# Attention and two feed-forward stages in one kernel: blocks in product order, sums last in a step, conversions in two calls, next-stage loads from the third product

## The chip, the cores and the metric

The kernel runs on one core of a Trainium2 chip. The metric is the device time of one execution in microseconds. Three runs of the kernel before gave 1167.41, 1167.29 and 1166.38 us; the median is 1167.29.

## The reference

Attention with normalised q and k over 4 x 12 heads of 448 x 64, then two feed-forward stages on the same 1792 tokens of width 768. All weights of the two stages are given in double precision (float64).

```python
q_n, k_n = (rmsnorm(q, g_q), rmsnorm(k, g_k))
scores = scale * np.matmul(q_n, k_n.transpose(0, 1, 3, 2))
scores = scores - np.max(scores, axis=-1, keepdims=True)
attn = np.exp(scores)
attn = attn / (np.sum(attn, axis=-1, keepdims=True) + 1e-09)
x = np.matmul(attn, v)                      # then (1792, 768)
# stage 0: w_in 768 x 2048, w_out 2048 x 768
h = np.maximum(x @ w_in, 0.0)
x = (h * h) @ w_out
# stage 1: w_gate and w_val 768 x 1536, w_out 1536 x 768
g = x @ w_gate
silu = g * (1.0 / (1.0 + np.exp(-g)))
out = (silu * (x @ w_val)) @ w_out
```

## The kernel before

After the attention come four stages of matmuls: up 0 and down 0 (the two matrices of the first feed-forward stage), up 1 and down 1. In each, a product of two block matrices is made from seven block products P1 to P7 in place of eight (Strassen's scheme, in the form of Winograd), with sums and differences of blocks on both sides. Every 32-bit block is split into a high and a low half of the fp32r type, and a block product is three matmuls: high by high, high by low, low by high.

- **up(ph)** works in steps of 9 matmuls. A step is one product, one pair of hidden blocks q_ and one half of the tokens (tp). q_ = 0 and 1 are interleaved (28 steps), later q_ take 14 steps each, in the order P1, (P4 of the one before), P5, P6, P2, P7, P3. up 0 has 112 steps, up 1 168.
- **down(ph)** goes through the products in the order P2, P5, P3, P1, P6, P7, P4, each over ng blocks of the hidden width (ng is 8 in stage 0 and 6 in stage 1), with 18 matmuls per block n. At a product's last block its six banks are copied or added out (L1301 for copies).
- **Weight blocks** go through a ring of five buffers (`ring`; in the trace without numbers, in the order of instructions as ring_82 to ring_86). stream() makes them: ACT casts the high half (L494), DVE subtracts for the low half (L267). Sums of blocks that a product needs are made in `ssum`, `conv` or in place (plus L270, minus L267).
- **Conversions**: weights arrive as 768 KB slabs of double-precision words (loads, L250, in three regions of xacc) and are turned into 32-bit floats by convert(): one ACT instruction (L291), a TENSOR_SCALAR (L292) and two SCALAR_TENSOR_TENSOR (L264) on DVE. Quads feed up stages. Slabs for a down stage ("keep") are converted during the up stage, stored to memory (`wkeep`, L354) and fetched back by bring() (dn<-wkeep, L363); some ("area") are converted straight into `dn` when the down stage has begun.
- **Hidden blocks**: finished sums are stored by send_part() (hid<-xacc, L1018), in the down stages fetched by stage() (dn<-hid, L1224) and split by cleave(): ACT the high half (L1237), DVE the low half (L1059, xat or xab<-dn). sum_of() makes further sums of hidden blocks on DVE (L1059, xacc<-xacc).
- **Order on an engine** is the order of emission; each engine runs its queue in order. After each step, pump(rate) issues conversions (C), blocks (B) and low halves that are due (L) until a budget of DVE time is spent. run_due() runs what later() has planned; load_raws() issues loads up to `state["limit"]`. At the start of up 0 a table given to plan_types() places splits ("h" ACT L146, "l" DVE L150) and combines ("c" L127) of the two token pairs' input blocks. All DMAs here are issued by SP's queue, in order.

## Time and profile before

| | |
|---|---|
| median of three runs | 1167.29 us |
| lowest and highest | 1166.38 and 1167.41 us |
| the profiled execution, its own time | 1166.46 us |
| its span | 1164.4 us |
| mean granted clock of TensorE | 0.988 of full speed |
| PE busy | 1127.7 us (97%) |
| DVE busy | 869.5 us (75%) |
| ACT busy | 636.9 us (55%) |
| POOL busy | 213.0 us (18%) |
| slabs loaded (w_in, w_out, w_gate, w_val) | 16, 28, 12, 12 (768 KB each) |
| wkeep stores and reads | 23 and 23 (384 KB each) |

The profile comes from one execution, whose own time is near the lowest of the three runs; the span leaves out some 2 us around it. w_out stands for both second matrices. PE is busy nearly all the time, so the time lies in the few places where PE stands still, or runs its matmuls at a lower clock, and in what it waits for there. The column PEclk of a window is the granted clock as a share of full speed.

### The profile page before, as it was taken

To read this page: it belongs to the slowest core of one execution; us is meant where nothing else is said; L and a number is where in the kernel's file an instruction comes from. 1 tells how busy PE (TensorE), PEld (TensorE's weight loads), DVE (VectorE), ACT (ScalarE), POOL (GpSimd) and SP (SyncE) were. 2 spreads that over 40 slices of the span, in tenths; PEclk is the share of its full clock that TensorE was granted. 3 is DMA by queue.
4 is the path that set the end of the run, shared out by engine and by line. 5 is a ranking of instruction groups with operands and counts; after the bars stand their busy time and mean duration, and the time that the engine had idled before them with its cause. 6 is when DMAs were issued, how large, how long until landed. Compare 5 with 4: busy or idle time off the path is not lost.

```text
span 1164.4 us, 17032 instructions
## 1 busy us (share of the span) xinstructions
PE 1127.7 (97%) x6164; PEld 953.7 (82%) x6164; DVE 869.5 (75%) x1253; ACT 636.9 (55%) x1047; POOL 213.0 (18%) x220
## 2 busy tenths in 40 slices
PE   7999999999799999789999999999999999999998
PEld 5555555569699899679999999999999899898997
DVE  7777888679878887789456787979787784765554
ACT  6887877667566665554444546443443434245332
POOL 5899999741000000000000000000000000000000
PEclk9999999999999999899999999999999999999999
DMA  6444332111978778984444401755464551764553
GB/s 172 122 123 125 97 97 60 47 33 35 323 238 266 248 245 281 355 292 143 127 127 127 127 17 51 242 173 194 146 219 144 185 183 50 279 231 131 174 177 136
DMA packets 116739, 190.38 MB, mean 164 GB/s; under 512 B 13616, under 2 KB 97584, under 8 KB 116656
## 3 DMA queue, kind: packets, MB, share of 16 engines
q1 hardware_dynamic: 116336, 189.30, 50.5%
q8 instruction: 48, 0.79, 0.3%
q14 instruction: 35, 0.29, 0.1%
q10 hardware_dynamic: 320, 0.00, 0.0%
HBM read 129.50 MB, written 59.59 MB: 162 GB/s over the span
## 4 chain that ended last, share of the span: by engine, by line
PE 74%; DVE 10%; DMA 9%; ACT 3%; issue 2%; SPq 1%; POOL 0%; ACTq 0%; DVEq 0%; POOLq 0%
PE ps L1097 31%; PE ps L1278 25%; PE s L750 6%; PE s L765 6%; DMA dn<-wkeep 3%; DVE xacc L1059 3%; PE s L721 2%; DVE conv L264 2%; PE s L689 2%; PE s L786 2%; DMA hid<-xacc 2%; DMA dn<-hid 1%; DMA xacc<-in_moe_w_out_dram 1%; DVE ring L267 1%; ACT xacc L1062 1%
## 5 line engine op out<-in xcount | busy, mean ns | idle before, releaser
L1097 PE MATMUL ps<-xb,ring 128*128 128x448 f32 x1080 | 231.7, 371 | 9.9 <-DVE ring L267 9.1
L1097 PEld LDWEIGHTS ps<-xb,ring 128*128 128x128 f32 x1080 | 205.4, 191 | 29.7 <-DVE ring L267 11.7
L1278 PE MATMUL ps<-xat,ring 128*128 128x448 f32 x1008 | 211.0, 372 | 11.1 <-DVE xat L1059 5.9
L1278 PEld LDWEIGHTS ps<-xat,ring 128*128 128x128 f32 x1008 | 192.6, 192 | 29.4 <-DVE xat L1059 7.9
L1278 PE MATMUL ps<-xab,ring 128*128 128x448 f32 x756 | 155.9, 368 | 2.8 <-ACT xacc L1301 1.8
L1097 PE MATMUL ps<-xat,ring 128*128 128x448 f32 x720 | 156.1, 366 | 0.8 <-DVE ring L267 0.8
L1278 PEld LDWEIGHTS ps<-xab,ring 128*128 128x128 f32 x756 | 143.0, 190 | 15.5 <-ACT xacc L1301 2.2
L1097 PEld LDWEIGHTS ps<-xat,ring 128*128 128x128 f32 x720 | 135.0, 188 | 12.5 <-DVE ring L267 1.1
L1062 ACT ACTIVATE xacc<-ps 128x448 f32<-128x448 f32 x148 | 79.3, 543 | 102.7 <-PE ps L1097 95.4
L264 DVE SCALAR_TENSOR_TENSOR conv<-xacc,conv 128x768 int32<-128x768 int32 x126 | 121.5, 965 | 3.3
L1062 ACT ACTIVATE xacc<-xacc 128x448 f32<-128x448 f32 x148 | 84.8, 577 | 68.9 <-DVE xacc L1059 66.7
L1097 PE MATMUL ps<-xab,ring 128*128 128x448 f32 x540 | 116.3, 366 | 0.0
L1059 DVE TENSOR_TENSOR xacc<-ps,xacc 128x448 f32<-128x448 f32 x164 | 98.5, 619 | 20.0 <-PE ps L1097 14.5
L724 DVE TENSOR_REDUCE mxz<-s 112x2 f32<-112x896 f32 x96 | 100.2, 1088 | 16.4 <-PE s L721 16.1
L1097 PEld LDWEIGHTS ps<-xab,ring 128*128 128x128 f32 x540 | 101.3, 188 | 8.8 <-issue 0.7
L1237 ACT CAST xat<-dn 128x896 fp32r<-128x896 f32 x56 | 52.8, 943 | 96.3 <-PE ps L1278 66.0
L1059 DVE TENSOR_TENSOR xat<-dn,xat 128x896 fp32r<-128x896 f32 x56 | 61.0, 1089 | 55.3 <-ACT xat L1237 55.0
L756 POOL TENSOR_TENSOR sg<-p 112x896 f32<-112x896 f32 x46 | 96.8, 2106 | 15.1 <-ACT p L752 15.1
L752 ACT ACTIVATE p<-s 112x896 f32<-112x896 f32 x96 | 87.8, 919 | 20.4 <-PE s L750 16.1
L267 DVE TENSOR_TENSOR ring<-conv,ring 128x384 fp32r<-128x384 f32 x127 | 69.7, 559 | 30.2 <-ACT ring L494 30.1
L1059 DVE TENSOR_TENSOR xacc<-xacc 128x448 f32<-128x448 f32 x148 | 87.6, 620 | 4.5 <-DMA hid<-xacc 4.0
L1059 DVE TENSOR_TENSOR xab<-dn,xab 128x896 fp32r<-128x896 f32 x42 | 45.8, 1090 | 52.4 <-ACT xab L1237 52.4
(97 smaller groups left out, 1353.4 us busy)
## 6 DMA issues: line engine op xcount, KB each, us to landing
hid<-xacc SPq DMA_DIRECT2D x196, 224.0 KB
dn<-hid SPq DMA_DIRECT2D x98, 448.0 KB
xacc<-in_moe_w_out_dram SPq DMA_DIRECT2D x28, 768.0 KB
xacc<-in_moe_w_in_dram SPq DMA_DIRECT2D x16, 768.0 KB
xacc<-in_moe_w_gate_dram SPq DMA_DIRECT2D x12, 768.0 KB
xacc<-in_moe_w_val_dram SPq DMA_DIRECT2D x12, 768.0 KB
wkeep<-conv SPq DMA_DIRECT2D x23, 384.0 KB
dn<-wkeep SPq DMA_DIRECT2D x23, 384.0 KB
```

Source lines behind the costliest of these rows:

```text
L264: nc.vector.scalar_tensor_tensor(out=out, in0=in0, scalar=scalar, in1=out, op0=op, op1=ALU.bitwise_or)
L267: nc.vector.tensor_tensor(out=out, in0=a, in1=b, op=ALU.subtract)
L724: nc.vector.tensor_reduce(out=mxz[:, c, 0:P:D], in_=ps[:CP, :, :S], op=ALU.max, axis=AX.X)
L750: nc.tensor.matmul(ps[:CP, a, :S], lhs, rhs, start=(w == 0), stop=(w == 3))
L752: nc.scalar.activation(out=p, in_=ps[:CP, :, :S], func=AF.Exp)
L756: nc.gpsimd.tensor_tensor(out=sg, in0=p_t[pi, 2 * w], in1=p_t[pi, 2 * w + 1], op=ALU.add)
L765: nc.tensor.matmul(ps[s, :S], v_t[pi][:, a, c * D:(c + 1) * D], p[:, a, :], start=(c == 0), stop=(c == NCH - 1),)
L1059: eng.tensor_tensor(out=o, in0=a, in1=b, op=op)
L1062: nc.scalar.activation(out=slot(s), in_=src, func=func)
L1097: nc.tensor.matmul(ps, w[:, wi, kk * P:(kk + 1) * P], xk[:, xi, kk * S:(kk + 1) * S], start=bool(first and mm == 0), stop=(mm == 3 * KT - ...
L1237: nc.scalar.copy(k[:, 0], src)
L1278: nc.tensor.matmul(ps_of(ps[tp, o]), w[:, wi, o * P:(o + 1) * P], h[:, hi, tp * S:(tp + 1) * S], start=bool(first and m == 0), stop=(g == ...
```

## The change

It changes the order in which work is issued, and which slabs are kept.

- In stage 0 the kept even slabs are one (0) instead of three (0, 2, 4), so 9 slabs are stored and brought instead of 11, and slabs 2 and 4 become area slabs. The table `more`, by which kept slabs are spread over q_, changes with it.
- The limit of the loads: in up 0 all loads of stage 0 are open from the first step (before, after the table of splits is done); in down 0 the loads of the next stage's first quads (four) are open from block 2 x ng on, the first of the third product.
- convert() issues the TENSOR_SCALAR one call of pump later than the ACT part.
- stream() makes P6's block before P2's, as the products use them.
- Sums by sum_of() are issued at the end of a step, after pump.
- In a down stage, at a product's last block the evictions are issued ahead of pump and of the low half of the hidden block n + 2. bring() asks for slabs up to n + 7 in place of n + 5.
- The table of plan_types for up 0 has the splits of T3 and B21 of pair two ahead of those of T4 of pair one.

```diff
@@ -199,14 +199,15 @@
     loads, limits, jobs, kepts = [], [], [], []
     for ph in range(2):
         nq = len(ups[ph])
-        kept = list(range(1, NF[ph], 2)) + list(range(0, (6, NF[1])[ph], 2))
+        kept = list(range(1, NF[ph], 2)) + list(range(0, (2, NF[1])[ph], 2))
         kepts.append(list(kept))
-        more = ({4: 1, 7: 4}, {7: 1, 11: 1})[ph]
+        more = ({2: -1, 5: 1, 6: 1, 7: 2}, {7: 1, 11: 1})[ph]
 
         def job(what, a, b, src):
             jobs.append((ph, what, a, b, len(loads)))
             loads.append(src)
 
+        limits.append(len(loads))
         for n, (w, g) in enumerate(ups[ph]):
             if n == 2:
                 limits.append(len(loads))
@@ -289,8 +290,10 @@
             high, low = two[:, :, 1], two[:, :, 0]
         ci = c.bitcast(I32)
         yield act(lambda: nc.scalar.activation(out=c, in_=high.bitcast(F32), func=AF.Copy, scale=TINY))
+        t = state["tick"]
         yield dve(0.56, lambda: nc.vector.tensor_scalar(
-            out=ci, in0=ci, scalar1=3, scalar2=0x7FFFFFFF, op0=ALU.logical_shift_left, op1=ALU.bitwise_and))
+            out=ci, in0=ci, scalar1=3, scalar2=0x7FFFFFFF, op0=ALU.logical_shift_left, op1=ALU.bitwise_and),
+            soft=lambda: state["tick"] > t)
         yield dve(0.97, stt, ci, high, -0x80000000, ALU.bitwise_and)
         yield dve(0.97, stt, ci, low, 29, ALU.logical_shift_right)
         turned[i] = clock["n"]
@@ -440,8 +443,8 @@
                     yield dve(0.55, minus, a21, a11, a21)
                     yield from block((ph, "P5", q_), s_, "s")
                     yield dve(0.55, minus, a11, a22, a21, gate=idle_(key(q_, "a11")))
+                    yield from block((ph, "P6", q_), a11, key(q_, "a11"))
                     yield from block((ph, "P2", q_), a12, key(q_, "a12"), since=lambda: -1)
-                    yield from block((ph, "P6", q_), a11, key(q_, "a11"))
                     yield from block((ph, "P7", q_), a21, key(q_, "a21"), since=lambda: -1)
                     yield dve(0.55, minus, a12, a12, a11, gate=idle_(key(q_, "a12")))
                     yield from block((ph, "P3", q_), a12, key(q_, "a12"), done=over(q_, 0))
@@ -1006,6 +1009,14 @@
         def later(n, fn, *args):
             due.append((clock["n"] + n, fn, args))
 
+        sums_due = []
+
+        def run_sums():
+            now = [d for d in sums_due if d[0] <= clock["n"]]
+            sums_due[:] = [d for d in sums_due if d[0] > clock["n"]]
+            for _, args in now:
+                sum_of(*args)
+
         def run_due():
             now = [d for d in due if d[0] <= clock["n"]]
             due[:] = [d for d in due if d[0] > clock["n"]]
@@ -1052,7 +1063,7 @@
                                      ("T2", ("B22", "T1"), 3 + end), ("T4", ("B21", "T2"), 2)):
                 if new not in when and all(x in when for x in needs):
                     t = when[new] = max(when[x] for x in needs) + wait
-                    later(t - now, sum_of, ph, g, tp, new)
+                    sums_due.append((t, (ph, g, tp, new)))
                     later(t - now + 3, send_part, ph, g, tp, new)
 
         def tt(eng, o, a, b, op=ALU.add):
@@ -1166,6 +1177,7 @@
                 cleave(tp, 0)
                 stage(ph, 2 + tp)
             pump(rate)
+            run_sums()
             if last and p == "P4":
                 cleave(tp, 1)
 
@@ -1188,8 +1200,7 @@
             run_types()
             for p, q_, tp in todo:
                 step(ph, p, q_, tp, 1.2, q_ == last)
-                if not types:
-                    state["limit"] = len(loads) if ph else limits[1]
+                state["limit"] = len(loads) if ph else limits[2]
                 if q_ == last and tp == 1:
                     level = {"P1": 0, "P6": 1, "P2": 2, "P3": 3, "P7": 4, "P4": 5}.get(p)
                     if level is not None:
@@ -1261,7 +1272,7 @@
                 w = ring[at[ph, p, -1 - g] % RING]
                 h = hbuf[n % 3]
                 if n == ng - 1:
-                    assert not due
+                    assert not due and not sums_due
                     free.clear()
                 if n < ng and not state["third"] and all(s in free for s in (3, 4, 5, 6)):
                     claim_third()
@@ -1286,8 +1297,9 @@
                 cleave(n + 2, 0)
                 run_due()
                 stage(ph, n + 4)
-                pump(rate / 2)
-                cleave(n + 2, 1)
+                if g < ng - 1:
+                    pump(rate / 2)
+                    cleave(n + 2, 1)
                 if g == ng - 1:
                     if ph == 0 and p == "P6":
                         assert not waiting((0, 1))
@@ -1312,11 +1324,17 @@
                                 i, j = {"P1": (0, 0), "P6": (0, 1), "P7": (1, 1), "P4": (1, 0)}[p]
                                 k_, t = i * KT + o, 2 * tp + j
                                 nc.sync.dma_start(out=out[k_ * P:(k_ + 1) * P, t * S:(t + 1) * S], in_=d)
-                bring(ph, n + 5)
+                bring(ph, n + 7)
+                if ph == 0 and n == 2 * ng:
+                    state["limit"] = limits[3]
                 load_raws()
                 for fn in plan.get(n, ()):
                     fn()
+                if g == ng - 1:
+                    cleave(n + 2, 1)
+                    pump(rate / 2)
                 pump(rate / 2)
+                run_sums()
             if ph == 0:
                 dn.clear()
                 xb.close()
@@ -1335,8 +1353,8 @@
             (0, "h", 1, "B11", None), (0, "l", 1, "B11", None), (1, "c", 1, "T1", None), (1, "h", 1, "T1", None),
             (2, "l", 1, "T1", None), (3, "h", 0, "T2", None), (4, "l", 0, "T2", None), (5, "h", 1, "B22", None),
             (6, "l", 1, "B22", None), (7, "c", 1, "T3", None), (8, "c", 1, "T2", None), (9, "h", 1, "T2", None),
-            (10, "l", 1, "T2", None), (10, "h", 0, "T4", None), (11, "l", 0, "T4", None), (12, "h", 1, "T3", None),
-            (13, "l", 1, "T3", None), (14, "h", 1, "B21", None), (15, "l", 1, "B21", None), (16, "c", 1, "T4", None),
+            (10, "l", 1, "T2", None), (10, "h", 1, "T3", None), (11, "l", 1, "T3", None), (12, "h", 1, "B21", None),
+            (13, "l", 1, "B21", None), (14, "c", 1, "T4", None), (15, "h", 0, "T4", None), (16, "l", 0, "T4", None),
             (17, "h", 1, "T4", None), (18, "l", 1, "T4", None),
         ])
         up(0)
```

The first place is on DVE at the start of up 0, where xb and xat are split halves of the input blocks and ring_85, ring_86 and ring_82 the blocks of steps 5 and later. Right ahead of the first row stands another subtraction in the kernel before, and the L150 split of xb in the changed one. Before:

```order
L267 TENSOR_TENSOR conv_76<-conv_77 128x384
L150 TENSOR_TENSOR xb_3387<-xacc,xb_3387 128x1344
L267 TENSOR_TENSOR ring_85<-ssum,ring_85 128x384
L267 TENSOR_TENSOR ssum<-conv_76 128x384
L267 TENSOR_TENSOR conv_79<-conv_78,conv_79 128x384
L267 TENSOR_TENSOR conv_78<-conv_79 128x384
L150 TENSOR_TENSOR xb_3387<-xacc,xb_3387 128x1344
L810 RECIPROCAL sp<-sp 56x16
L267 TENSOR_TENSOR ring_86<-ssum,ring_86 128x384
L267 TENSOR_TENSOR ssum<-conv_78 128x384
L150 TENSOR_TENSOR xat<-xacc,xat 128x1344
L267 TENSOR_TENSOR ring_82<-ssum,ring_82 128x384
```

The same place in the changed kernel:

```order
L268 TENSOR_TENSOR conv_76<-conv_77 128x384
L268 TENSOR_TENSOR ring_85<-ssum,ring_85 128x384
L268 TENSOR_TENSOR ssum<-conv_76 128x384
L150 TENSOR_TENSOR xb_3386<-xacc,xb_3386 128x1344
L813 RECIPROCAL sp<-sp 56x16
L268 TENSOR_TENSOR conv_79<-conv_78,conv_79 128x384
L268 TENSOR_TENSOR conv_78<-conv_79 128x384
L268 TENSOR_TENSOR ring_86<-ssum,ring_86 128x384
L268 TENSOR_TENSOR ssum<-conv_78 128x384
L150 TENSOR_TENSOR xat<-xacc,xat 128x1344
L127 TENSOR_TENSOR xacc<-xacc 128x1344
L268 TENSOR_TENSOR ring_82<-ssum,ring_82 128x384
```

The subtractions that stood ahead of a split now stand between it and the low half of the ring, and a combine (L127) stands ahead of ring_82.

The second place is on DVE at steps 24 to 30 of up 0; ring_83 is P6's block, ring_84 P2's, conv_77 a slab in conversion. Before:

```order
L1059 TENSOR_TENSOR xacc<-xacc 128x448 x3
L267 TENSOR_TENSOR conv_80<-conv_76 128x384
L1059 TENSOR_TENSOR xacc<-xacc 128x448 x2
L267 TENSOR_TENSOR ring_82<-ssum,ring_82 128x384
L1059 TENSOR_TENSOR xacc<-xacc 128x448 x3
L292 TENSOR_SCALAR conv_77<-conv_77 128x768
L264 SCALAR_TENSOR_TENSOR conv_77<-xacc,conv_77 128x768 x2
L1059 TENSOR_TENSOR xacc<-xacc 128x448 x2
L267 TENSOR_TENSOR ring_84<-conv_80,ring_84 128x384
L292 TENSOR_SCALAR conv_78<-conv_78 128x768
L264 SCALAR_TENSOR_TENSOR conv_78<-xacc,conv_78 128x768
```

The same place in the changed kernel:

```order
L268 TENSOR_TENSOR conv_80<-conv_76 128x384
L1070 TENSOR_TENSOR xacc<-xacc 128x448 x2
L268 TENSOR_TENSOR ring_82<-ssum,ring_82 128x384
L294 TENSOR_SCALAR conv_77<-conv_77 128x768
L265 SCALAR_TENSOR_TENSOR conv_77<-xacc,conv_77 128x768 x2
L1070 TENSOR_TENSOR xacc<-xacc 128x448 x5
L268 TENSOR_TENSOR ring_83<-conv_80,ring_83 128x384
L1070 TENSOR_TENSOR xacc<-xacc 128x448 x3
L268 TENSOR_TENSOR ring_84<-conv_80,ring_84 128x384
L1070 TENSOR_TENSOR xacc<-xacc 128x448 x2
```

The low half of ring_82 and the conversion move ahead of the sums, ring_83's low half comes ahead of ring_84's, and the conversion of conv_78 falls behind both.

The third place is on DVE in down 1, from block 2 to block 5; `plus` makes the sums in ssum and conv for P5's blocks, and xab<-dn is the low half of a hidden block. Before:

```order
L270 TENSOR_TENSOR conv_80<-dn 128x384
L1059 TENSOR_TENSOR xab<-dn,xab 128x896
L267 TENSOR_TENSOR ring_84<-ssum,ring_84 128x384
L1059 TENSOR_TENSOR xacc<-xacc 128x448
L1059 TENSOR_TENSOR xab<-dn,xab 128x896
L267 TENSOR_TENSOR ring_85<-conv_80,ring_85 128x384
L1059 TENSOR_TENSOR xab<-dn,xab 128x896
L270 TENSOR_TENSOR ssum<-dn 128x384
L1059 TENSOR_TENSOR xab<-dn,xab 128x896
```

The same place in the changed kernel:

```order
L271 TENSOR_TENSOR conv_78<-dn 128x384
L1070 TENSOR_TENSOR xab<-dn,xab 128x896
L268 TENSOR_TENSOR ring_84<-ssum,ring_84 128x384
L1070 TENSOR_TENSOR xacc<-xacc 128x448 x2
L271 TENSOR_TENSOR ssum<-dn 128x384
L1070 TENSOR_TENSOR xab<-dn,xab 128x896
L268 TENSOR_TENSOR ring_85<-conv_78,ring_85 128x384
L1070 TENSOR_TENSOR xacc<-xacc 128x448
L271 TENSOR_TENSOR conv_78<-dn 128x384
L1070 TENSOR_TENSOR xab<-dn,xab 128x896
```

The plus into ssum moves ahead by two of the low halves (xab<-dn), and another plus follows ahead of the next.

## Rows read from the trace of the kernel before

**Rows 1.** The page, part 1: busy time of each engine.
```profile
PE 1127.7 (97%) x6164; PEld 953.7 (82%) x6164; DVE 869.5 (75%) x1253; ACT 636.9 (55%) x1047; POOL 213.0 (18%) x220
```
**Rows 2.** Windows: length, busy time (instructions) of each engine, PEclk, DMA share, GB/s.
```profile
285.00:325.00 40.00, 33.31 (x149) 29.38 (x148) 29.82 (x49) 24.65 (x46) 0.00 (x0) 0.91 0.85 288
...
467.00:515.00 48.00, 36.94 (x151) 31.38 (x150) 36.15 (x51) 25.48 (x40) 0.00 (x0) 0.86 1.01 352
...
900.00:950.00 50.00, 47.55 (x228) 43.63 (x227) 38.01 (x63) 19.87 (x37) 0.00 (x0) 0.97 0.52 166
1002.00:1055.00 53.00, 50.20 (x237) 45.29 (x236) 39.82 (x64) 25.35 (x43) 0.00 (x0) 0.97 0.73 257
```
**Rows 3.** Timeline of PE: start, length, instructions, [idle before them and what ended it].
```profile
254.81 3.81 PE L1097 MATMUL ps<-xb,ring 128*128 128x448 f32 x18
...
284.00 3.81 PE L1097 MATMUL ps<-xb,ring 128*128 128x448 f32 x18
...
317.61 5.74 PE L1097 MATMUL ps<-xb,ring 128*128 128x448 f32 x16 [5.08 <-DVE ring L267]
...
398.11 3.51 PE L1097 MATMUL ps<-xb,ring 128*128 128x448 f32 x16 [1.40 <-DVE ring L267]
...
472.16 1.46 PE L1278 MATMUL ps<-xat,ring 128*128 128x448 f32 x2 [4.87 <-ACT ring L494]
...
508.90 11.38 PE L1278 MATMUL ps<-xat,ring 128*128 128x448 f32 x47 [3.56 <-DVE xat L1059]
...
904.70 12.37 PE L1097 MATMUL ps<-xb,ring 128*128 128x448 f32 x52 [2.45 <-DVE ring L267]
...
1003.46 44.08 PE L1278 MATMUL ps<-xab,ring 128*128 128x448 f32 x214 [0.97 <-DVE ring L267]
1049.32 10.95 PE L1278 MATMUL ps<-xab,ring 128*128 128x448 f32 x45 [1.78 <-ACT xacc L1301]
```
**Rows 4.** Waits of PE for one releaser: total us, times, longest.
```profile
PE ps L1278 <- DVE xat L1059: 5.9, 4, 3.6
```
**Rows 5.** The page, part 5: busy us, mean ns | idle before.
```profile
L264 DVE SCALAR_TENSOR_TENSOR conv<-xacc,conv 128x768 int32<-128x768 int32 x126 | 121.5, 965 | 3.3
...
L1059 DVE TENSOR_TENSOR xat<-dn,xat 128x896 fp32r<-128x896 f32 x56 | 61.0, 1089 | 55.3 <-ACT xat L1237 55.0
...
L1059 DVE TENSOR_TENSOR xacc<-xacc 128x448 f32<-128x448 f32 x148 | 87.6, 620 | 4.5 <-DMA hid<-xacc 4.0
```
**Rows 6.** Timeline of DVE at the start of up 0.
```profile
259.91 0.55 DVE L267 TENSOR_TENSOR ring<-ssum,ring 128x384 fp32r<-128x384 f32 x1
...
267.01 0.55 DVE L267 TENSOR_TENSOR ring<-ssum,ring 128x384 fp32r<-128x384 f32 x1
267.48 4.05 DVE L127 TENSOR_TENSOR xacc<-xacc 128x1344 f32<-128x1344 f32 x2
```
**Rows 7.** Timeline of POOL in the same stretch.
```profile
268.95 1.17 POOL L821 TENSOR_TENSOR xacc<-xu,rb 128x448 f32<-128x448 f32 x1 [4.34 <-DMA rb<-row]
```
**Rows 8.** Timeline of DVE in up 0, around step 32.
```profile
311.00 0.56 DVE L292 TENSOR_SCALAR conv<-conv 128x768 int32<-128x768 int32 x1 [1.93 <-ACT conv L291]
...
317.00 0.55 DVE L267 TENSOR_TENSOR ring<-conv,ring 128x384 fp32r<-128x384 f32 x1
```
**Rows 9.** Timeline of ACT at the end of up 0.
```profile
458.68 0.89 ACT L291 ACTIVATE conv<-xacc 128x768 f32<-128x768 f32 x1 [2.78 <-DVE ring L267]
```
**Rows 10.** Timeline of SP's queue before down 0 and in down 1.
```profile
464.35 0.60 SPq L363 DMA_DIRECT2D dn<-wkeep  x1
...
1016.15 0.49 SPq L1224 DMA_DIRECT2D dn<-hid  x1
...
1021.06 0.89 SPq L363 DMA_DIRECT2D dn<-wkeep  x1
```
**Rows 11.** Timeline of DVE: plus for P5 in down 0 and in down 1.
```profile
505.81 0.56 DVE L270 TENSOR_TENSOR ssum<-dn 128x384 f32<-128x384 f32 x1 [4.15 <-DMA dn<-wkeep]
...
1027.20 0.56 DVE L270 TENSOR_TENSOR ssum<-dn 128x384 f32<-128x384 f32 x1 [3.42 <-DMA dn<-wkeep]
```
**Rows 12.** Timeline of ACT at the end of the second product of down 1.
```profile
1048.32 0.51 ACT L494 CAST ring<-dn 128x384 fp32r<-128x384 f32 x1 [2.11 <-DVE dn L267]
```

## Prediction

> **What bounds the kernel now.** I read the share of each engine, then windows of 40 to 55 us, then PE's timeline around the windows that lose time, and last the engines that PE waits for there. PE is busy for 97% of the span [rows 1], so this is a search for the few places where it is not. From 254.81 to 284.00 PE runs 144 matmuls without a wait [rows 3]: 29.19 / 144 = 0.2027 us each. A window's loss is its length less its matmuls at that price [rows 2]: 40.00 - 149 x 0.2027 = 9.8 us in the middle of the first up stage, 48.00 - 151 x 0.2027 = 17.4 at the start of down 0, 3.8 late in the second up stage, and 53.00 - 237 x 0.2027 = 5.0 in the first two products of down 1. With a single wait of 1.40 at 398.11 [rows 3] that is 37.4 us; all else lies under 4 us.
>
> What PE waits for in them is the same each time: a low half made by DVE, or an ACT cast or copy that stands behind something waiting on DVE [rows 3]. A wait also costs something behind it. After the waits at 508.90, 904.70 and 1049.32 the runs of 47, 52 and 45 matmuls take 11.38, 12.37 and 10.95 us, so 1.85, 1.83 and 1.83 more than at 0.2027 [rows 3]; the granted clock in the windows around them is 0.86 to 0.97 [rows 2], a fall from the higher level (2.4 GHz) to the lower (1.2) for a few us after PE stood still. After 0.97 us at 1003.46 the run of 214 loses only 0.7. So I price a new wait at its length plus 1.8 when it is over some 1.5 us, and plus 0.2 to 0.5 when it is below 1.
>
> **Order of blocks, two-call conversions, sums last (up stages).** At step 28 the DVE queue before holds five sums and a conversion ahead of P2's low half, and P6's low half, needed first, behind P2's. The conversion's first DVE instruction is queued right behind the ACT part and waits for it, 1.93 us at 311.00; the low that PE waits 5.08 us for at 317.61 starts at 317.00 [rows 3, 8]. The change adds no instruction here. It swaps P2 and P6, so that P6's block is made in the order of use, delays the TENSOR_SCALAR by one pump, and puts sums behind lows. If I lay the durations of the trace on the new order (0.56 a low, 0.62 a sum, 0.56 + 2 x 0.965 a conversion [rows 5, 8, 11]) the lows come 2 to 4 us before PE needs them. The sums are now late by a low or two, 1.1 us; their reader is the send three steps on, and nobody waits for that here. The first load of the next slabs now goes out at step 14 instead of 18, so data for the later conversions isn't late either. Loss 9.8 -> 0.2 (bounds 0 and 3: one conversion of 2.5 plus a low left in the way). The same cause stands behind 398.11 and 904.70, both waits on a ring low [rows 3], where the P6 block is now made six steps ahead and not three: 1.4 -> 0 (to 1.4) and 3.8 -> 0.3 (0 to 2).
>
> **Splits of pair two and sums at the very start.** This costs. The low half ring_85 (259.91, 0.55) now has two subtractions between it and the split ahead of it that were done earlier before: + 2 x 0.5, so it ends at 261.5 [rows 6]. PE needs it 29 matmuls after 254.81, at 254.81 + 29 x 0.2027 = 260.69 [rows 3]: 0.8 us of wait. The low half ring_82 (267.01) now stands behind the first of the two combines, which take 4.05 together [rows 6], and one plus of 0.56 more is ahead: 267.01 + 0.5 + 2.0 + 0.5 = 270.0. PE wants it 65 matmuls after 254.81, at 268.0: 2.0, of which 0.8 are already lost, so 1.3 more. With 0.5 for the clock: 2.6 us (0.5 if DVE's idle times absorb the earlier shift, 3.6 if the combine is the slow one). That choice matters because POOL runs a tensor-tensor on the same data at 268.95 for 1.17 us, within these combines [rows 7].
>
> The Trainium skill, page "SBUF — State Buffer", section "Who interferes with whom", says that a DVE instruction with two SBUF inputs and a GpSimd instruction that reads SBUF lock each other out for the whole instruction. Nothing in the rows above says which of the two came first. By that rule the low would be up to 1.17 us later and the term 3.8 instead of 2.6; the sum goes by the row.
>
> **Kept slabs, limits, next stage's loads (start of down 0).** Before, two conversions still run in the last steps of up 0: ACT waits 2.78 us ahead of one at 458.68 [rows 9], the sum of the hidden blocks waits 4.0 for its DMA [rows 5], and the first bring leaves SP only at 464.35 [rows 10]; PE then stands 4.87 us at 472.16 [rows 3]. Of the 17.4 us I count 4.9 for this wait, 3.56 + 1.85 = 5.4 for that at 508.90, 5.9 - 3.56 = 2.3 for three other waits on the low half of a hidden block [rows 4], and the remaining 4.8 for the clock. The change keeps 9 slabs instead of 11 (two stores and two reads of wkeep less), and no conversion is left after step 98. The end of up 0 then looks like the end of up 1, which has none either, and where PE waits 0.97 us [rows 3]: 1.4 with the clock.
>
> Then DVE. In the first 16 steps (eight blocks, 144 matmuls, 29.2 us of PE) it had 8 low halves of hidden blocks, 7 sums, 8 TENSOR_SCALARs, 15 SCALAR_TENSOR_TENSORs and 11 pluses and minuses: 8 x 1.09 + 7 x 0.62 + 8 x 0.56 + 15 x 0.965 + 11 x 0.56 = 38.2 us [rows 5, 8, 11]. Now it has 8, 7, 7, 13 and 15: 37.8, since two slabs more are converted in place of the next stage's quads, which move to the third product. In the window DVE is busy 36.15 for 51 instructions [rows 2], 0.71 each where the sum gives 0.78, since neighbours overlap: 37.8 x 0.91 = 34.4, or 5.2 us more than PE. I take 4.1 of it as lost, since one low half may still be open at the end. The plus that waited 4.15 us for its slab ahead of a low half [rows 11] now finds it earlier, since its bring leaves at the third block and not the fifth. Total 1.4 + 4.1 = 5.5 (2.5 to 12). The next stage's loads run past nothing that waits: their data is wanted some 80 steps later.
>
> **Brings two blocks earlier, evictions before the last split (down 1).** The copy of the second product's banks no longer stands behind the cast that waits 2.11 us for DVE [rows 12], and PE's 1.78 + 1.83 at 1049.32 [rows 3] go: -3.6. In exchange the plus of P5's first block moves from the sixth block to the fourth, ahead of the low half of block 5. Its slab's bring can leave SP only behind the stage at 1016.15 [rows 10], at some 1016.5. Before, the same plus waited until 1027.20 for a bring of SP's that left at 1021.06 (the third column shows 3.42 of wait) [rows 10, 11], 6.1 us; I allow 5 to 6. So it lands at 1021.6 to 1022.6, the low half is done 0.56 + 1.09 later, at 1023.3 to 1024.3, and PE wants it 89 matmuls after 1003.46 [rows 3], at 1021.5: 1.8 to 2.8, and 1.8 for the clock, so 4.1 (0 to 5). With the 1.3 of the start, 5.0 -> 5.4.
>
> **The sum.** Gains 9.6 + 1.4 + 11.9 + 3.5, costs 0.4 + 2.6: 23.4 us. The profiled execution took 1166.46, so 1143.1; the median of the three runs is 0.83 above it. I put the forecast, rounded, at 1143.
>
> **Rivals.** (A) The start of down 0 stays bound by DVE: 34.4 against 29.2 us of PE [rows 2], with each of several short waits followed by the lower clock. For it: the low half is late in four places before [rows 4]. Against: the two long waits had causes that go. Then it loses 12 instead of 5.5: 1150. (B) The two new waits don't come, since DVE has slack at the start and the bring lands in 4 us: 2.6 + 4.1 less, 1136. (C) The gain of one place is given back: conversions that no longer stand ahead of lows come late themselves, and a later block waits for its slab. Half of 9.6 + 11.9 back: 1154. (D) No change: the waits move by a step and keep their length, since DVE's work is the same in sum; only 398.11 goes: 1165. (E) Slower: a plus queued ahead of the low half waits for its bring each time. The place is the second product of both down stages, 14 pluses, of which some 12 follow a bring or an area. At the price of 508.90, 3.56 + 1.85 = 5.4 us each [rows 3], that is 65 us, less the 23.4: 1208. Five such waits undo the whole gain; it decides when brings land later than their low half is wanted at five blocks or more. Against it: only one bring is left behind the start in down 0.
>
> **How the numbers follow.** Forecast, 1137 to 1149: 0.58. A, to 1153: 0.14. B, 1130 to 1137: 0.11. C, 1153 to 1165: 0.07. D: 0.05. E: 0.05. A change of 0.2% (2.3 us) is about the least that a measurement of this kernel can tell. Faster 0.90, the same 0.05, slower 0.05. The range 1134 to 1156 leaves out half of B and of C, D and E, 0.19.
>
> **What would show it.** Right: no wait on a ring low between 300 and 320 us; the wait at the first matmul of down 0 near 1 us and the first bring right behind PE's last read; new waits of 1 us or less near 261 and 268; DVE's conversion instructions without waits for ACT; ACT's copies of the second product of down 1 directly behind its last matmul, and a wait of about 2 us some 20 us into down 1, with a plus ahead of it that waits for wkeep. Wrong: four or more waits on a low half of a hidden block between the first and the ninth block of down 0 (A or E), or waits of ACT's conversions on their loads (C).

## The result, and the profile after

The changed kernel takes 1148.2 us (median of 4 runs, 1144.98 to 1153.92) against 1167.17 (4 runs, 1166.38 to 1167.41) before: a ratio of 0.9844, with a 95% interval of 0.9804 to 0.9884. It is faster, by some 19 us where 24 were forecast. The profiled execution took 1147.27 us. The page of it, part 1:

```profile
span 1145.5 us, 17038 instructions
...
PE 1118.6 (98%) x6164; PEld 947.9 (83%) x6164; DVE 872.7 (76%) x1253; ACT 638.6 (56%) x1047; POOL 214.3 (19%) x220
```

DVE is as busy as before (869.5 us); PE is busy for 9 us less, though it makes the same matmuls: fewer of them ran at the lower clock, and some 50 us of the kernel before ran at the higher of the two prices that the last section shows. The windows of the changed kernel that answer to those of [rows 2], in the same columns:

```profile
250.00:285.00 35.00, 32.30 (x158) 27.12 (x155) 27.45 (x29) 18.19 (x28) 8.13 (x5) 0.95 0.07 21
285.00:325.00 40.00, 40.00 (x199) 37.08 (x198) 36.35 (x59) 30.47 (x56) 0.00 (x0) 1.00 0.80 257
465.00:515.00 50.00, 45.14 (x211) 40.30 (x210) 45.34 (x67) 26.27 (x40) 0.00 (x0) 0.97 0.83 282
900.00:950.00 50.00, 50.00 (x249) 46.33 (x248) 40.72 (x68) 21.58 (x41) 0.00 (x0) 1.00 0.51 171
984.00:1037.00 53.00, 49.65 (x242) 44.76 (x241) 39.28 (x62) 26.74 (x43) 0.00 (x0) 1.00 0.72 247
```

Up 0 runs without a gap in the second window (199 matmuls in 40 us, 149 before) and up 1 in the fourth (249 in 50, 228 before). The first window is a new loss, the third and the fifth still have one: 50 - 211 x 0.2027 = 7.2 us and 53 - 242 x 0.2027 = 3.9. The rows of PE's timeline with the larger waits of the feed-forward stages:

```profile
263.56 1.68 PE L1108 MATMUL ps<-xat,ring 128*128 128x448 f32 x7 [0.72 <-DVE ring L268]
273.10 1.80 PE L1108 MATMUL ps<-xab,ring 128*128 128x448 f32 x7 [1.98 <-DVE ring L268]
463.05 0.47 PE L1289 MATMUL ps<-xat,ring 128*128 128x448 f32 x1 [0.67 <-ACT ring L497]
...
478.24 9.21 PE L1289 MATMUL ps<-xat,ring 128*128 128x448 f32 x36 [3.00 <-DVE xat L1070]
487.92 3.91 PE L1289 MATMUL ps<-xat,ring 128*128 128x448 f32 x18 [0.48 <-DVE xat L1070]
492.85 3.91 PE L1289 MATMUL ps<-xat,ring 128*128 128x448 f32 x18 [1.02 <-DVE xat L1070]
497.13 178.82 PE L1289 MATMUL ps<-xat,ring 128*128 128x448 f32 x881 [0.36 <-DVE xat L1070]
983.56 7.17 PE L1289 MATMUL ps<-xab,ring 128*128 128x448 f32 x34 [0.77 <-DVE ring L268]
...
1005.67 135.41 PE L1289 MATMUL ps<-xab,ring 128*128 128x448 f32 x665 [2.42 <-DVE xab L1070]
```

Between 273 and 463 us, between 497 and 983, and after 1006 no wait of 0.3 us or more is left. The waits of [rows 3] at 317.61, 398.11, 904.70 and 1049.32 are gone, that of 4.87 at the first block of down 0 is 0.67.

To compare kernels whose stages lie at different times, I add up, over PE's timeline, what each step from one matmul's start to the next takes beyond 0.2027 us, where it takes more than 0.215; waits and matmuls at the lower clock both count. By place, in us (the last column takes in the end of the second product of down 1):

| kernel | first 15 steps of up 0 | rest of up 0 | first 2 products of down 0 | up 1 | start of down 1 | sum |
|---|---|---|---|---|---|---|
| before | 0.1 | 11.7 | 17.6 | 5.5 | 5.2 | 40.0 |
| changed | 4.9 | 0.0 | 9.2 | 0.0 | 5.5 | 19.6 |
| changed, once more | 3.4 | 0.0 | 9.5 | 0.0 | 7.6 | 20.5 |
| changed, conversions in one call | 0.1 | 5.8 | 14.0 | 0.0 | 5.9 | 25.8 |
| changed, old order of P2 and P6 | 3.2 | 0.7 | 10.3 | 0.7 | 5.5 | 20.3 |
| changed, sums first | 3.4 | 0.0 | 6.3 | 0.0 | 5.5 | 15.1 |
| changed, old table of splits | 2.5 | 0.0 | 9.8 | 0.0 | 6.0 | 18.3 |
| changed, 11 kept slabs | 4.9 | 0.0 | 15.5 | 0.0 | 4.2 | 24.6 |
| changed, old brings and evictions | 4.7 | 0.0 | 11.3 | 0.0 | 7.6 | 23.7 |
| before, P6 ahead of P2 | 0.1 | 4.4 | 19.1 | 0.0 | 3.3 | 27.0 |
| before, conversions in two calls | 3.3 | 1.7 | 15.1 | 3.8 | 4.7 | 28.6 |
| before, limits of loads | 0.1 | 10.8 | 15.4 | 5.1 | 3.2 | 34.6 |
| three edits to the changed | 0.1 | 0.0 | 6.8 | 0.0 | 2.1 | 9.0 |
| four edits to the changed | 0.1 | 0.0 | 3.8 | 0.0 | 2.8 | 6.7 |

The sum is what to read here, more than the times: runs of one kernel lie up to 17 us apart, for a reason of which the last section shows a part, while the sum came out as 19.6 and 20.5 in two profiles of the changed kernel.

### The profile page after: what moved, and what is told of

Its sections match the earlier page's. It is cut to its first block, busy times and chain, and to the rows that moved or that the text cites. A ratio compares the mean times of both kernels' runs of the same rounds, so it can differ in the third digit from the quotient of the medians.

```text
span 1145.5 us, 17038 instructions
## 1 busy us (share of the span) xinstructions
PE 1118.6 (98%) x6164; PEld 947.9 (83%) x6164; DVE 872.7 (76%) x1253; ACT 638.6 (56%) x1047; POOL 214.3 (19%) x220
## 4 chain that ended last, share of the span: by engine, by line
PE 84%; DMA 5%; DVE 4%; POOL 2%; issue 2%; ACT 1%; SPq 1%; DVEq 0%; POOLq 0%; ACTq 0%
PE ps L1108 42%; PE ps L1289 26%; PE s L768 5%; PE s L753 5%; DMA dn<-wkeep 2%; PE s L724 2%; PE s L692 2%; PE s L789 1%; DMA dn<-hid 1%; POOL sg L759 1%; POOL qk L674 1%; PE s L733 1%; DVE mxz L727 1%; DMA hid<-xacc 1%; DMA raw<-in_k_dram 1%
## 5 line engine op out<-in xcount | busy, mean ns | idle before, releaser
L1108 PE MATMUL ps<-xb,ring 128*128 128x448 f32 x1080 | 225.4, 365 | 0.0
L1108 PEld LDWEIGHTS ps<-xb,ring 128*128 128x128 f32 x1080 | 202.8, 188 | 16.0
L1070 DVE TENSOR_TENSOR xacc<-ps,xacc 128x448 f32<-128x448 f32 x164 | 100.9, 621 | 42.5 <-PE ps L1108 25.7
L265 DVE SCALAR_TENSOR_TENSOR conv<-xacc,conv 128x768 int32<-128x768 int32 x122 | 117.8, 965 | 3.6
L759 POOL TENSOR_TENSOR sg<-p 112x896 f32<-112x896 f32 x46 | 99.1, 2155 | 14.9 <-ACT p L755 14.9
L1248 ACT CAST xab<-dn 128x896 fp32r<-128x896 f32 x42 | 39.6, 944 | 87.3 <-PE ps L1289 60.0
```

The costliest lines, as they stand in the source:

```text
L265: nc.vector.scalar_tensor_tensor(out=out, in0=in0, scalar=scalar, in1=out, op0=op, op1=ALU.bitwise_or)
L759: nc.gpsimd.tensor_tensor(out=sg, in0=p_t[pi, 2 * w], in1=p_t[pi, 2 * w + 1], op=ALU.add)
L1070: eng.tensor_tensor(out=o, in0=a, in1=b, op=op)
L1108: nc.tensor.matmul(ps, w[:, wi, kk * P:(kk + 1) * P], xk[:, xi, kk * S:(kk + 1) * S], start=bool(first and mm == 0), stop=(mm == 3 * KT - ...
L1248: nc.scalar.copy(k[:, 0], src)
```

## The experiments

**Conversions back in one call.** Edit to the changed kernel:

```diff
-            out=ci, in0=ci, scalar1=3, ...), soft=lambda: state["tick"] > t)
+            out=ci, in0=ci, scalar1=3, ...))
```

> The changed kernel with one part undone: the TENSOR_SCALAR of a conversion is again issued in the same call as its ACT part. Theory 1 (the two calls shift the chain of blocks by one unit of the attention, so that ring_85 and ring_82 come late at the start of up 0): the waits of 0.72 at 263.56 and 1.98 at 273.10 and the lower clock behind them (4.9 us together) are gone, up 0 to up 1 lose 0 to 3 us at conversions that wait for ACT: 1142 to 1147 us. Rival (DVE standing behind ACT was what made the low halves late in up 0): waits on ring lows of 3 to 8 us come back between 300 and 330 us: 1150 to 1156 us.

1153.2 us (10 runs, 1148.61 to 1165.67), ratio to before 0.9896 (0.9861 to 0.9930). The time is the rival's (1150 to 1156). Of theory 1 the first half came true: the start of up 0 lost nothing. Of the rival, up 0 lost time again, 5.8 us, but in waits for ACT and not on ring lows (PE's timeline of this kernel):

```profile
314.69 2.08 PE L1106 MATMUL ps<-xb,ring 128*128 128x448 f32 x9 [1.46 <-ACT xacc L1071]
319.07 3.60 PE L1106 MATMUL ps<-xb,ring 128*128 128x448 f32 x9 [2.29 <-ACT xacc L1071]
...
477.21 13.88 PE L1287 MATMUL ps<-xat,ring 128*128 128x448 f32 x54 [2.88 <-DVE xat L1068]
494.84 188.53 PE L1287 MATMUL ps<-xat,ring 128*128 128x448 f32 x917 [3.75 <-DVE xat L1068]
```

ACT's L1071 empties the banks that PE needs. ACT's timeline shows it standing still for 3.83 us ahead of that:

```profile
318.47 0.54 ACT L1071 ACTIVATE xacc<-ps 128x448 f32<-128x448 f32 x1 [3.83 <-issue]
```

"issue" is waiting for nothing that the profile shows, so what was late there stays open. Just before, DVE's TENSOR_SCALAR stood 1.31 us for ACT at 314.23, and the sums queued behind that conversion ended at 318.39, 0.08 us ahead of this row; that ACT waited for them is not shown. In down 0 the loss grew from 9.2 to 14.0. So two calls help in up 0 and in down 0 and cost at the start.

**P2 ahead of P6 again.**

```diff
-                    yield from block((ph, "P6", q_), a11, key(q_, "a11"))
                     yield from block((ph, "P2", q_), a12, key(q_, "a12"), since=lambda: -1)
+                    yield from block((ph, "P6", q_), a11, key(q_, "a11"))
```

> The changed kernel with one part undone: P2's block is made before P6's again. Theory 1 (P6's block came too late because it was made behind P2's): waits on ring lows come back near 308 to 320 us, near step 74 (1 to 2 us) and late in up 1 (2 to 4 us with the clock), 5 to 12 us in all: 1153 to 1160 us. Rival (sums last and two calls are enough by themselves, the order of two blocks doesn't matter): no wait above 0.5 us between 300 and 900 us, 1146 to 1150 us.

1148.7 us (4 runs, 1143.94 to 1151.88). The rival came true: two waits of 0.4 us came back, one in up 0 and one in up 1, 1.3 us in all. With the other parts in place the order of the two blocks is nearly free; that it matters by itself shows only below.

**Sums ahead of pump again.**

```diff
-                    sums_due.append((t, (ph, g, tp, new)))
+                    later(t - now, sum_of, ph, g, tp, new)
```

> The changed kernel with one part undone: sums of hidden blocks are issued ahead of pump again. Theory 1 (sums ahead of lows made the lows late): 1 to 3 us of waits on ring lows between 305 and 320 us, and 1 to 3 us more on low halves of hidden blocks in the first five blocks of down 0: 1150 to 1154 us. Rival (sums sent earlier let the hidden blocks be stored and fetched earlier, and DVE idles less at the start of down 0, 2.0 us there now): the wait of 3.00 at 478.24 shrinks, 1143 to 1147 us.

1150.4 us (4 runs, 1144.39 to 1152.83), but 15.1 us of loss and not 19.6: in the profiled execution some 500 us of it ran at the higher price of a matmul (last section). The losses are the rival's: up 0 has no wait with sums first either, and the wait at the fourth block of down 0, ahead of its 56th matmul (the expectations call that block the third), nearly goes:

```profile
463.79 12.73 PE L1289 MATMUL ps<-xat,ring 128*128 128x448 f32 x53 [0.54 <-DVE ring L268]
477.11 15.54 PE L1289 MATMUL ps<-xat,ring 128*128 128x448 f32 x72 [0.58 <-DVE xat L1070]
```

But PE had not lost less by then: 4.6 us of down 0's loss lie up to this matmul, where the changed kernel has 4.9. Here the lower clock came earlier, in the 53 matmuls of the first row (12.73 us, where the changed kernel's 54 take 11.47), so PE reached the wait later. The gain comes after it, 1.7 us of loss in place of 4.3: no lower clock of 1.7 us behind a long wait, and no waits of 0.48 and 1.02. Down 0 loses 2.9 us less in this one profile; so sums last in a step, which the prediction counted among the gains, cost time there.

**The old table of splits and combines.**

```diff
-(10, "h", 1, "T3"), (11, "l", 1, "T3"), (12, "h", 1, "B21"), (13, "l", 1, "B21"), (14, "c", 1, "T4"), (15, "h", 0, "T4"), ...
+(10, "h", 0, "T4"), (11, "l", 0, "T4"), (12, "h", 1, "T3"), (13, "l", 1, "T3"), (14, "h", 1, "B21"), (15, "l", 1, "B21"), ...
```

> The changed kernel with one part undone: the old table of splits and combines at the start of up 0. Theory 1 (the table is not what makes the start lose time; the first ten steps have the same order of instructions with either table): the waits of about 0.7 and 2.0 us near 263 and 273 us stay, the time is within 4 us of 1148. Rival (the prediction's naming: the table's new order puts a combine ahead of ring_82's low half): both waits go, 1143 to 1145 us. The first load behind it moves to a later step, with a wait of up to 2 us near 310 us by either.

1154.8 us in one run, more than the 4 us around 1148 that were expected; some 490 us of it ran at the higher price of a matmul, which is 9 us (last section). Both waits stayed, 0.72 and 1.11 us:

```profile
263.02 1.68 PE L1108 MATMUL ps<-xat,ring 128*128 128x448 f32 x7 [0.72 <-DVE ring L268]
271.69 1.68 PE L1108 MATMUL ps<-xab,ring 128*128 128x448 f32 x7 [1.11 <-DVE ring L268]
```

The table isn't the cause; one call removed them, so two calls are. By the code, every conversion made during the attention lies one call later, the chain of blocks with it, and up 0 begins with ring lows still to make. The first version below bears this out: it puts back into one call the conversions of the attention alone, and loses 0.1 us at the start. The second wait is shorter here for another reason, shown in the last section.

**Single parts on the kernel before.** P6 ahead of P2 alone, two calls alone, and the limits of the loads alone (the edits are those of the change):

> The kernel before with one part of the change alone: P6's block is made before P2's. Theory 1 (the prediction's: P6's block came too late because it was made behind P2's): of the 10 us lost between 305 and 322 us at least 5 go, and the waits at 398 (1.4 us) and 904 (2.5 us) go: 1155 to 1161 us. Rival (undoing this part alone brought back only about 1 us, so another part does the work): the waits near 317 and 398 us stay within 1 us of what they were, 1163 to 1168 us.

> The kernel before with one part of the change alone: conversions in two calls. Theory 2 (DVE standing behind ACT's part of a conversion made the low halves late, and undoing this part gave back 5.8 us in up 0): the 10 us lost between 305 and 322 us fall to 2 to 5, while the start of up 0 loses 2 to 5 us in two waits near 262 and 271: 1160 to 1165 us. Rival (the parts work only together): the up-0 loss stays above 7 us and the start's waits come on top, 1167 to 1172 us.

> The kernel before with one part of the change alone: the limits of the loads (all of stage 0 open from the first step of up 0, the next stage's first quads only from the third product of down 0). Theory 3 (the slabs come too late, and the quads' loads and conversions fill the DMA queues and DVE at the start of down 0): the loss in up 0 falls by 3 to 8 us and that in the first 16 steps of down 0 (12.6 us) by 3 to 6: 1153 to 1160 us. Rival (order on DVE is the cause, loads are early enough): both stay within 1.5 us, 1163 to 1168 us.

The three took 1157.9, 1154.9 and 1168.9 us in one run each, beside 1176.0 in one run of the kernel before on that chip. The window from 300 to 330 us tells most, first of the kernel before, in the columns of [rows 2]:

```profile
300.00:330.00 30.00, 23.31 (x100) 20.11 (x99) 23.48 (x42) 15.63 (x31) 0.00 (x0) 0.89 0.84 293
```

Then with P6 ahead of P2:

```profile
300.00:330.00 30.00, 28.20 (x136) 24.87 (x134) 25.47 (x45) 16.29 (x32) 0.00 (x0) 1.00 0.91 304
```

with two calls:

```profile
300.00:330.00 30.00, 28.77 (x142) 26.34 (x142) 27.44 (x48) 18.35 (x35) 0.00 (x0) 1.00 0.93 316
```

and with the limits:

```profile
300.00:330.00 30.00, 22.98 (x103) 20.32 (x102) 25.92 (x43) 17.53 (x33) 0.00 (x0) 0.89 0.93 312
```

By 30 - x * 0.2027 these lose 9.7, 2.4, 1.2 and 9.1 us. The order of blocks and the two calls each take most of the same 9.7 us, and that is why undoing the order alone gave so little back; loads that are open earlier take almost none. In up 1 the order alone took all of 5.5 us; two calls took away the wait of [rows 3] at 904.70 but brought one of 1.98 at 792.70, and 3.8 us stayed. Two calls alone also brought the two waits at the start. The limits alone took 2.2 us in the first two products of down 0 (17.6 to 15.4), where the theory had 3 to 6, and their own first wait there was 6.72 us. No run has sums last alone on the kernel before.

**11 kept slabs again.**

```diff
-        kept = list(range(1, NF[ph], 2)) + list(range(0, (2, NF[1])[ph], 2))
+        kept = list(range(1, NF[ph], 2)) + list(range(0, (6, NF[1])[ph], 2))
-        more = ({2: -1, 5: 1, 6: 1, 7: 2}, {7: 1, 11: 1})[ph]
+        more = ({4: 1, 7: 4}, {7: 1, 11: 1})[ph]
```

> The changed kernel with one part undone: 11 kept slabs of stage 0 again, with the old table of when they are loaded. Theory (the two conversions in the last steps of up 0 delayed the first brings, and PE's 4.87 us at the first block of down 0 with them): a wait of 3 to 5 us returns at the first block of down 0, with the lower clock behind it 5 to 8 us more: 1152 to 1158 us. Rival (the earlier loads alone let all conversions end in time): the wait stays below 1.5 us, and with two area conversions less on DVE the next blocks lose 1 to 3 us less: 1144 to 1149 us.

1156.1 us in one run. The theory came true, with the first wait a little under its 3 to 5 us. PE's timeline:

```profile
466.58 14.46 PE L1289 MATMUL ps<-xat,ring 128*128 128x448 f32 x55 [2.91 <-ACT ring L497]
481.68 7.86 PE L1289 MATMUL ps<-xat,ring 128*128 128x448 f32 x36 [0.64 <-DVE xat L1070]
492.77 9.51 PE L1289 MATMUL ps<-xat,ring 128*128 128x448 f32 x36 [3.23 <-DVE xat L1070]
504.79 178.82 PE L1289 MATMUL ps<-xat,ring 128*128 128x448 f32 x881 [2.51 <-DVE xat L1070]
```

The first wait is back at 2.91 (4.87 before), with others behind it: 15.5 us against 9.2. Two slabs fewer to keep are worth 6 us at this place, the largest of down 0's gains among the parts undone here.

**Old brings and old evictions, in one kernel.**

```diff
-                bring(ph, n + 7)
+                bring(ph, n + 5)
-                if g < ng - 1:
-                    pump(rate / 2)
-                    cleave(n + 2, 1)
+                pump(rate / 2)
+                cleave(n + 2, 1)
-                if g == ng - 1:
-                    cleave(n + 2, 1)
-                    pump(rate / 2)
                 pump(rate / 2)
```

> The changed kernel with two parts undone that meet in down 1: brings up to n + 5, and evictions behind pump and the low half of the next hidden block. Theory (the earlier plus makes the wait of 2.42 us at the sixth block, and the copies behind a waiting cast made the 1.78 us at the end of the second product): the wait at the sixth block goes, a wait of 1.5 to 2.5 us for ACT's copies returns some 36 matmul steps of 18 later than the start of down 1 (at its 216th matmul); down 1 loses 3 to 5 us as now; in down 0 the wait for a low half at the sixth block returns (2 to 4 us): 1147 to 1154 us. Rival (the copies' wait was made by the conversions' or sums' order): no wait of PE for ACT's copies, down 1 loses under 2 us.

1151.9 us in one run. PE's timeline in down 1:

```profile
1012.22 18.57 PE L1289 MATMUL ps<-xab,ring 128*128 128x448 f32 x89 [1.27 <-DVE xab L1070]
1033.24 113.36 PE L1289 MATMUL ps<-xab,ring 128*128 128x448 f32 x540 [2.45 <-ACT xacc L1312]
```

The wait at the sixth block moved to the eighth, where its plus now stands, and fell to 1.27; that for ACT's copies returned with 2.45, at the same matmul as in [rows 3]. So the two edits together account for both waits. Which edit does which is argued from the places in the queues, since both were undone at once: ACT's copies stand again behind a cast that waits for DVE (2.10 us), as in [rows 12], and the plus moves with its bring. Down 1 lost 7.6 us, more than the 3 to 5 expected. In down 0 a wait of 2.51 for a low half came back, not at the sixth block but at the eighth, ahead of the same matmul as that of [rows 3] at 508.90; the first two products lost 11.3 us in place of 9.2.

**The changed kernel once more, and two versions of it.**

> The changed kernel once more, to see how far its profile repeats. Theory (its order of work fixes its waits): about 0.7 and 2.0 us at the start of up 0, 3 us at the third block of down 0 and 2.4 us at the sixth of down 1 appear again within 1 us, and the sum of what PE loses to waits and to the lower clock is 18 to 22 us; the first matmul of up 0 starts anywhere between 251 and 255 us and a part of the stages may run at 0.2067 us for a matmul instead of 0.2027: 1145 to 1154 us. Rival (the profile on record was a lucky one): another 5 us or more of waits, or the first matmul always 2 us later than before.

1147.05 us (4 runs, 1142.12 to 1148.69), ratio 0.9821 (0.9781 to 0.9862). All waits came back within 0.5 us of their first values (0.72, 1.99, 0.66, 2.80, 2.86).

The first version makes three edits to the changed kernel:

```diff
-            soft=lambda: state["tick"] > t)
+            soft=lambda: state["used"] == 0 or state["tick"] > t)
-                    sums_due.append((t, (ph, g, tp, new)))
+                    later(t - now, sum_of, ph, g, tp, new)
-                bring(ph, n + 7)
+                bring(ph, n + 9)
```

> The changed kernel with three edits: in the attention conversions stay in one call, sums are issued ahead of pump as before, and slabs are brought up to n + 9 in place of n + 7. Theory (the waits left come from these three): the waits at the start of up 0 (4.9 us with the clock) and at the sixth block of down 1 (2.4) go, and the first blocks of down 0 lose 4 to 6 us instead of 8.4; PE loses 8 to 11 us in all instead of 19.6: 1136 to 1143 us, 8 us or more below the changed kernel on the same chip. Rival (DMA at the start of a down stage is full, and a bring that leaves earlier delays the stages of hidden blocks): the wait moves to the first four blocks of down 0 and down 1, 1145 to 1150 us.

1147.4 us (4 runs, 1140.04 to 1151.67), ratio 0.9827 (0.9776 to 0.9877). The losses went nearly as the theory said, 9.0 us in all (6.8 in the first blocks of down 0, where 4 to 6 were expected), the time did not: nearly the whole profiled execution ran at the higher price of a matmul, which cost 16 us, more than the 10.6 that the edits won. Which price the other three runs had no profile shows. One wait stood out:

```profile
477.87 15.54 PE L1289 MATMUL ps<-xat,ring 128*128 128x448 f32 x72 [3.11 <-DVE xat L1070]
```

There a low half stands behind two conversions of area slabs. The second version starts those one block later:

```diff
-        yield act(lambda: None, gate=lambda: state["step"] >= 100 * ph)
+        yield act(lambda: None, gate=lambda: state["step"] >= 100 * ph + 1)
```

> The kernel of best3 with one more edit: the conversions of area slabs begin one block later in a down stage. Theory (what is left in down 0 is a low half of a hidden block that stands on DVE behind two conversions, 3.3 us at the third block): that wait falls below 1.5 us, and PE loses 4 to 8 us in all to waits and the lower clock: 1134 to 1146 us by runs whose matmuls take 0.2027 or 0.2067 us, some 25 to 30 us below the kernel before on the same chip. Rival (DVE has 34 us of work for 29 us of PE there, so the wait moves): 3 us or more of waits appear between the fourth and the tenth block of down 0, and the sum stays at 9 to 11.

1138.6 us (6 runs, 1135.07 to 1153.17), ratio 0.9739 (0.9698 to 0.9780), better than the changed kernel's 0.9844 and 0.9821, each against the kernel before on its own chip; its interval ends just below where the nearer of the two begins (0.9781). The wait is gone; the rows with waits from down 0 on are now

```profile
464.96 0.47 PE L1289 MATMUL ps<-xat,ring 128*128 128x448 f32 x1 [0.63 <-ACT ring L497]
465.68 0.47 PE L1289 MATMUL ps<-xat,ring 128*128 128x448 f32 x1 [0.25 <-DVE xat L1070]
466.68 205.72 PE L1289 MATMUL ps<-xat,ring 128*128 128x448 f32 x1006 [0.53 <-DVE ring L268]
980.53 23.04 PE L1289 MATMUL ps<-xab,ring 128*128 128x448 f32 x112 [1.06 <-DVE ring L268]
1004.50 130.37 PE L1289 MATMUL ps<-xab,ring 128*128 128x448 f32 x642 [0.93 <-ACT xacc L1313]
```

## Why the prediction was right, and where it was wrong

The time lies in the range and the forecast's sign and main terms held, at 1148.2 for 1143.0. The terms expected 14.0 us of loss to stay, and 19.6 stayed: 2.3 more at the start of up 0, 3.7 more in down 0, 0.1 more in down 1 and 0.5 less in the up stages. The misses nearly all go one way, so no luck among the terms put the time into the range; it lies near the range's upper end. In the profiled executions the span fell by 18.9 us: 20.4 of losses and 1.1 because a stretch of the kernel before ran at the higher price of a matmul, less 2.0 because the first matmul of up 0 started at 253.05 instead of 251.05, and less 0.6 behind the last matmul. No run ties that start to the change: it lies between 251.05 and 255.76 in the profiles shown here, and at 254.16 in the kernel before with P6 ahead of P2, whose attention is that of before.

- **Up stages, 9.8, 1.4 and 3.8 to 0.2, 0 and 0.3: right**, all three are 0.0. Of the three parts named, two are shown, and each alone takes most of the loss in up 0. Sums last isn't needed: with the other two in place, sums first lose nothing there either. Whether it would have taken some of the loss alone no run shows; undoing the order of blocks gave back nearly as little, 0.7 us, and yet that order alone takes most. The earlier load alone took 0.9.
- **The start of up 0, 2.6: the cost was foreseen, its cause partly misnamed.** The prediction put it under the table of splits; the experiment on the table left both waits, the one on the calls removed them. The order of instructions had shown a pair of subtractions late and a combine ahead, and I didn't ask which edit had put them there. The prediction's sign was two waits of 1 us or less; the second was 1.98. The size, 4.9 and in the second profile 3.4, is larger by about 1 us for POOL in both, and in the first by 1.7 for the lower clock behind the second wait, where the prediction had 0.5 for the clock. DVE's low half, then POOL's operation, from the timelines of the changed kernel:

```profile
271.53 1.51 DVE L268 TENSOR_TENSOR ring<-ssum,ring 128x384 fp32r<-128x384 f32 x1
```

```profile
270.72 1.91 POOL L824 TENSOR_TENSOR xacc<-xu,rb 128x448 f32<-128x448 f32 x1 [4.11 <-DMA rb<-row]
```

  The low half began inside POOL's operation and took 1.51 us where it takes 0.55 elsewhere [rows 6]; it ended 0.4 us after POOL did. By the rule weighed in the prediction (the Trainium skill, "SBUF — State Buffer", section "Who interferes with whom": one waits for the whole instruction of the other) the term was 3.8. The trace agrees with it: the low half took 1 us longer. The clock fell behind the wait in one of the two profiles and not in the other.
- **The first block of down 0, 4.87 to 0.97: right**, 0.67, and by the cause given for the larger part: with 11 kept slabs it is 2.91. What took the rest, 4.87 to 2.91, no run separates.
- **DVE at the start of down 0, 4.1: the mis-sized term.** The whole place was put at 5.5 and is 9.2. I took DVE as evenly late. It is idle first, then late in a lump. DVE's timeline of the changed kernel:

```profile
469.64 1.09 DVE L1070 TENSOR_TENSOR xat<-dn,xat 128x896 fp32r<-128x896 f32 x1 [2.04 <-ACT xat L1248]
...
474.65 0.55 DVE L294 TENSOR_SCALAR dn<-dn 128x768 int32<-128x768 int32 x1
475.23 1.95 DVE L265 SCALAR_TENSOR_TENSOR dn<-xacc,dn 128x768 int32<-128x768 int32 x2
477.10 1.08 DVE L1070 TENSOR_TENSOR xat<-dn,xat 128x896 fp32r<-128x896 f32 x1
...
486.31 0.56 DVE L271 TENSOR_TENSOR ssum<-dn 128x384 f32<-128x384 f32 x1 [1.83 <-DMA dn<-wkeep]
```

  It waits 2.04 us for a hidden block (whose own DMA ACT waits for), then has two conversions ahead of the low half that PE needs: 3.00 us of PE's wait, and 1.7 for the clock. Conversions one block later remove it, as one edit to the first version (3.11 to none); sums first do not, since that version has them too. So the work on DVE would have fitted; its place in the queue didn't. The prediction's sign for rivals A and E, four or more waits on a low half between the first and the ninth block, came with five (0.25, 3.00, 0.48, 1.02 and 0.36): the place went part of the way to A, which put it at 12 and the time at 1150. The plus ahead of a low half also waited here, 1.83 us, for 0.48 of PE: rival E's mechanism, at one block.
- **Down 1, 5.0 to 5.4: right in sum and in place**, 5.5. The copies' wait is gone. The plus waits as worked out, for a bring that left at 997.73 (DVE's row, then SP's):

```profile
1004.06 0.56 DVE L271 TENSOR_TENSOR ssum<-dn 128x384 f32<-128x384 f32 x1 [3.52 <-DMA dn<-wkeep]
```

```profile
997.73 0.69 SPq L366 DMA_DIRECT2D dn<-wkeep  x1
```

  That is 6.3 us from issue to use, where I allowed 5 to 6; PE waited 2.42, within the 1.8 to 2.8 given.
- **1.8 us of lower clock behind each wait over 1.5: half right.** The price itself is nearer 1.7: a row's length takes in some 0.16 us of its last matmul (18 take 3.81 in [rows 3], and 3.65 from start to start). Counted over the 14 profiles, 33 of 45 waits that cost PE over 1.8 us were followed by the lower clock. Behind that at 1005.67 it didn't fall, nor behind 3.11 us in the first of the two versions; in the second profile of the changed kernel it did, in down 1. And it fell behind short waits too: with sums first, behind 0.66, 0.24 and 0.54 us at the start of down 0, where 0.2 to 0.5 was allowed for each below 1, it cost 1.8.

## What to carry to other kernels

When an order of instructions moves, find out for each edit alone what it moves, and read it at the place where a late instruction is waited for: here the part that gained most in one stage cost most in another, and two parts bought the same gain twice. An engine that has enough time in sum still makes others wait if long work stands ahead of short work that is wanted at once, so place the long work behind it, or a block later. And fetch what is used ahead of a critical instruction early enough for the time from issue to use that the trace shows.

## What the runs showed of the hardware

**A matmul has two prices at full granted clock.** From 600 to 700 us, without a wait in either, the changed kernel and the first version of it show

```profile
600.00:700.00 100.00, 100.00 (x495) 92.67 (x494) 75.05 (x88) 47.80 (x69) 0.00 (x0) 1.00 0.25 77
```

```profile
600.00:700.00 100.00, 100.00 (x486) 90.81 (x485) 74.14 (x88) 46.76 (x66) 0.00 (x0) 1.00 0.25 75
```

495 and 486 matmuls (those under way at the edges counted in), 0.2027 and 0.2067 us from start to start, at a granted clock of 1.00 in both. An execution changes from one price to the other for stretches of 50 to 700 us: the profile of before had the higher one from about 960 to 1010 us, that with sums first from about 490 to 985, that of the first version nearly throughout, which is 16 us. It doesn't come from the order of work: the kernel with the old table, whose edit ends in up 0, has the same instructions in the same order in the middle of up 1, and had the higher price there, where both profiles of the changed kernel had the lower. It is large enough for the spread of the first version, whose four runs lie 11.6 us apart at a granted clock of 0.999 to 1.0; which price they ran at is not shown. In the kernel before, whose runs lie from 1159.78 to 1175.97 on several chips, the granted clock varies as well, 0.994 in the shortest run and 0.987 in one of 1173.35, so part of that spread is time at the lower clock. What sets the price no row shows. Differences of a few us between kernels are therefore read from the losses, not from single times.

**POOL's and DVE's operations shift each other.** In the kernel with the old table POOL's operation came later, and the same low half took its 0.55 us. DVE's and POOL's rows there:

```profile
271.08 0.55 DVE L268 TENSOR_TENSOR ring<-ssum,ring 128x384 fp32r<-128x384 f32 x1
...
273.02 2.00 DVE L268 TENSOR_TENSOR ring<-conv,ring 128x384 fp32r<-128x384 f32 x2
```

```profile
271.77 2.37 POOL L824 TENSOR_TENSOR xacc<-xu,rb 128x448 f32<-128x448 f32 x1 [7.18 <-DMA rb<-row]
```

The wait there was 1.11 and not 1.98 because this low half kept its 0.55 us. The two low halves behind it, which began inside POOL's operation, took 2.00 us instead of 1.0.
